# Second-level factors of w_out formed on the chip in the first group of tokens, and two levels in all five products of the second group

## The chip, the cores and the metric

The kernel runs on one core of one Trainium2 chip. The metric is the device time of one execution in microseconds (us), as the median of several executions; lower is better. TensorE is called PE here, VectorE DVE, ScalarE ACT, GpSimd POOL and SyncE SP. Each engine takes its instructions in order. POOL and SP have little arithmetic in this kernel: they issue DMA transfers.

## The reference

The attention block turns q, k and v of shape (4, 8, 768, 64) into tokens x of shape (3072, 512). Two matrix products with a pointwise function between them follow:

```python
def reference(q, k, v, lam, moe_w_in, moe_w_out):
    attn_out = _attn_ref(q, k, v, lam)          # causal, decayed by lam ** distance, state carried from block to block
    x = attn_out.transpose(0, 2, 1, 3).reshape(B * S, H * D)     # (3072, 512)
    h = x @ moe_w_in                            # (512, 2048)
    g = h - np.tanh(h)
    return (g @ moe_w_out).astype(np.float32)   # (2048, 512)
```

Everything is float32 on the chip. The weights arrive as 64-bit floats and are rounded on the chip.

## The kernel before

**Groups.** The 3072 tokens are worked off in NG = 6 groups of 512 (128 positions of each of the 4 batches). Group 0 is the "first group" and group 1 the "second group". For each group there is an attention part (`att_transpose`, `att_scores`, `att_out`, `att_state`), the product with w_in ("up", four column blocks u = 0 to 3), and the product with w_out ("down"). The attention of group g + 1 is put in pieces between the up and down products of group g.

**Seven products instead of eight.** Up and down split their matrices in 2 x 2 blocks and use a seven-product scheme: sums and differences of blocks ("factors") are multiplied, and the products, numbered 1 to 7, are added up. For w_out the seven factors are B11, B21, B22 and the differences T1 to T4. One first-level down product is `down` at L644 to L685: 16 matmuls of 128x128 by 128x256 (the `nc.tensor.matmul` at L655). A "two-level" down product, `down_twice` at L697 to L730, applies the same scheme once more inside a product: seven sub-products of four matmuls of 128x128 by 128x128 (L708), 28 in all, with the sums of the hidden values made by `sums_twice` (L692 to L694) and the sums of w_out's factor made ahead of time. The function `twice(g, n)` says which products have two levels. Before the change these are products 5 and 6 in group 1, and 5, 6, 4, 7 and 3 in groups 2 to 4 (in group 5 all of these but 3).

**Where the factors lie.** w_out is loaded once, in pairs of 128-row blocks, kt = 0 to 7 (`weights`, `round_block`), at the end of group 0's up part and during its down part. For each kt `sums_out` (L252 to L267) makes T1, T2, T3 and T4 on DVE, stores all seven first-level factors to a DRAM tile `factors`, and stores those second-level factors that are plain slices (sub-products 1, 2 and 3) to a DRAM tile `fine`. The tile that holds a pair is one of two `wst` buffers or, for every third pair, `ws` tiles that group 0 does not need (`pair_tiles`). Sub-products 5, 6, 7 and 4 need differences between column halves and between rows of kt even and kt odd. They are made later: `load_quarters` fetches four quarters of a first-level factor from `factors`, and `factors_twice` (L603, L604) makes four 128x512 differences on DVE and stores each to `fine`. This happens for two of the five products between the steps of group 1's up part, and for the other three in group 2's up part.

**The stream of weights.** From group 1 on `piece` loads each factor piece (256 KB) from `factors` or `fine` by a DMA from POOL, RING = 7 pieces ahead.

**The pools that matter for the change.** The natural (token by channel) loads of k rotate through 3 buffers with tag "k" and those of v through 4 buffers with tag "v" in the pool `io`; SP issues them (L131). From group 2 on SP also issues q and k in blocks (L143), 16 transfers for each of the four batches and each of q and k, behind the natural loads on the same queue; DVE transposes them (L319). In the built program each DMA from POOL also waits until the eighth transfer before it on that queue has landed.

**Group 0's down part.** `down_first` (L792) walks over kt and adds all seven products of one pair in seven PSUM banks. `sums_late` (L798, L799) makes, on DVE, the two hidden sums that products 6 and 3 need, after products 1 and 2 of that kt have read the old values. Products 5, 4 and 7 stand between. Ahead of it the attention of group 1 for batches 2 and 3 runs: PE makes the scores (L340), DVE masks them into `ss` (L344), and PE makes `op` (L388, L394) and the state update `kv` (L362).

Of the kernel before, what the change touches and what calls it, by code (L numbers as in the profile page):

```python
# [9 lines left out]
F32 = mybir.dt.float32  # L10
# [6 lines left out]
AL = mybir.AluOpType  # L17
# [7 lines left out]
def kernel(  # L25
# [32 lines left out]
    nc = tc.nc  # L58
# [6 lines left out]
    NG = S // BLK  # L65
    HB = GRP // 2
    NU = DFF // 512
# [7 lines left out]
    io = ctx.enter_context(tc.tile_pool(name="io", bufs=4))  # L75
# [3 lines left out]
    opool = ctx.enter_context(tc.tile_pool(name="opool", bufs=4))  # L79
# [43 lines left out]
    raw, late = {}, {}  # L123
# [54 lines left out]

    ws = [wpool.tile([128, 3, 2, 256], F32, name=f"ws_{u}") for u in range(NU)]

    NX = 7
    factors = dram.tile([NX, 128, KH, 256], F32, name="factors")

    SUB = (1, 2, 6, 5, 7, 3, 4)
# [37 lines left out]
    def weights(n):  # L222

        while ready["done"] < min(n, len(blocks)):
            at_ = ready["done"]
            load_weights(at_ + WAHEAD)
            kind, n_, m = blocks[at_]
            if kind == "out" and m == 0:
                pair[n_] = pair_tiles(n_)
            w = w1[n_][:, m] if kind == "in" else pair[n_][0][:, 2 * m:2 * m + 2]  # L230
            if at_ in wraw:
                round_block(w, wraw.pop(at_), at_ < 2 * KI)
            else:
                load_block(nc.gpsimd, w, kind, n_, m)
            ready["done"] += 1

    def pair_tiles(kt):

        if kt % 3 == 2:
            return tuple(ws[u].rearrange("p x k c -> p (x k) c")[:, 0:4] for u in (3, 2))  # L240
        wt = wst.tile([128, 8, 256], F32, name="wt", tag="w")
        return wt[:, 0:4], wt[:, 4:8]

    def sums_in(u):
        a11, a12, a21, a22 = (w1[u][:, 2 * c:2 * c + 2, r] for r, c in ((0, 0), (0, 1), (1, 0), (1, 1)))
# [3 lines left out]
            tc.keep_in_program_order(nc.vector.tensor_tensor(dst, x, y, op=op))  # L249

    def sums_out(kt):
        bt, tt = pair[kt]  # L252
        b11, b12, b21, b22 = (bt[:, x] for x in range(4))
        t1, t2, t4, t3 = (tt[:, x] for x in range(4))
        nc.vector.tensor_tensor(t1, b12, b11, op=AL.subtract)
        nc.vector.tensor_tensor(t2, b22, t1, op=AL.subtract)
        nc.vector.tensor_tensor(t3, b22, b12, op=AL.subtract)
        nc.vector.tensor_tensor(t4, b21, t2, op=AL.subtract)
        f = factors[:].rearrange("x p k c -> p x k c")
        nc.gpsimd.dma_start(out=f[:, 0:1, kt, :], in_=bt[:, 0:1, :])  # L260
        nc.gpsimd.dma_start(out=f[:, 1:3, kt, :], in_=bt[:, 2:4, :])
        nc.gpsimd.dma_start(out=f[:, 3:NX, kt, :], in_=tt[:, 0:4, :])

        for x, j in ((1, 0),) if kt % 2 == 0 else ((2, 0), (3, 1)):
            dst = fine[:, SUB.index(x), :, kt // 2, :].rearrange("n p c -> p n c")
            nc.gpsimd.dma_start(out=dst[:, 0:1], in_=bt[:, 3:4, ts(j, 128)])
            nc.gpsimd.dma_start(out=dst[:, 1:5], in_=tt[:, 0:4, ts(j, 128)])  # L267

    def round_block(w, raw64, first):

# [276 lines left out]
    RING = 7  # L547

    def twice(g, n):
        return n in TWICE and not (g == NG - 1 and n == 3) and not (g == 1 and n in (4, 7, 3))  # L550

    def in_turn(g):

# [5 lines left out]
    def pieces_of(g):  # L559
        if g >= GI:  # L560
            yield from ((g, ("in", 4), x) for x in (6, 5, 3))
        if g == 2:
            yield from ((g, ("quarter", t), x) for t in (2, 3, 4) for x in range(4))
        for n in (1, 2, 4, 5, 6, 7):
            yield from ((g, n, x) for x in (SUB if twice(g, n) else range(NU)))
        if g == NG - 1:
            yield from ((g, 3, x) for x in range(NU))
            return
        for kind, x in in_turn(g):
            if kind == "down":  # L570
                yield g, 3, x
            elif x in (3, 5, 6):
                yield g + 1, ("in", 2), x
# [1 line left out]
    stream = [x for g in range(1, NG) for x in pieces_of(g)]  # L575
    sent = {"n": 0}

    MADE = (5, 6, 4, 7, 3)
    quarters = {}

    def quarter_source(t, i, j):
        return factors[XAT[FACT[MADE[t]][1]]].rearrange("p (u m) c -> p u m c", m=2)[:, :, i, ts(j, 128)]

    def load_quarters(t):

        for i in range(2):
            for j in range(2):
                if t > 1:
                    quarters[t, i, j] = piece(2, ("quarter", t), 2 * i + j).rearrange("p m (v c) -> p (m v) c", v=2)
                    continue  # L590
                if t == 0:
                    x = late["pool"].tile([128, NU, 128], F32, name="wq", tag="wb", bufs=RING)
                else:
                    x = opool.tile([128, NU, 128], F32, name="oq", tag="o")
                nc.gpsimd.dma_start(out=x, in_=quarter_source(t, i, j))
                quarters[t, i, j] = x

    def factors_twice(t):

        b11, b12, b21, b22 = (quarters.pop((t, i, j)) for i in range(2) for j in range(2))  # L600
        t1, t2, t4 = (late["pool"].tile([128, NU, 128], F32, name=f"wt{x}", tag="sums", bufs=4) for x in (1, 2, 4))
        for x, dst, a, b in ((5, t1, b12, b11), (6, t2, b22, t1), (7, b12, b22, b12), (4, t4, b21, t2)):
            tc.keep_in_program_order(nc.vector.tensor_tensor(dst, a, b, op=AL.subtract))  # L603
            nc.gpsimd.dma_start(out=fine[TWICE.index(MADE[t]), SUB.index(x)], in_=dst)  # L604
            yield

    def piece(g, n, x):

        i = stream.index((g, n, x))
        while sent["n"] < min(i + RING, len(stream)):  # L610
            g_, n_, x_ = stream[sent["n"]]
            t = late["pool"].tile([128, 2, 256], F32, name="wb", tag="wb", bufs=RING)
            if isinstance(n_, tuple) and n_[0] == "quarter":
                nc.gpsimd.dma_start(out=t.rearrange("p m (v c) -> p (m v) c", v=2),
                                    in_=quarter_source(n_[1], *divmod(x_, 2)))
            elif isinstance(n_, tuple):
                nc.gpsimd.dma_start(out=t.rearrange("p m c -> p (m c)"), in_=fine_in[
                    INNER.index(n_[1]), (5, 6, 3).index(x_)].rearrange("p u c -> p (u c)"))
            elif twice(g_, n_):
                nc.gpsimd.dma_start(out=t.rearrange("p m c -> p (m c)"),  # L620
                                    in_=fine[TWICE.index(n_), SUB.index(x_)].rearrange("p u c -> p (u c)"))
            else:
                nc.gpsimd.dma_start(out=t, in_=factors[XAT[FACT[n_][1]]][:, 2 * x_:2 * x_ + 2, :])  # L623
            blks[stream[sent["n"]]] = t
            sent["n"] += 1
        return blks.pop((g, n, x))
# [146 lines left out]

    acc = {}
    ACC = {1: ("ya", 1), 2: ("w", 1), 5: ("z", 1), 6: ("yb", 1), 7: ("att", 4), 4: ("att", 4), 3: ("att", 4)}
    FIRST = {1: (11, 0, 0), 2: (21, 0, 2), 3: (21, 0, 3), 4: (22, 1, 2), 5: ("S1", 1, 0), 6: (11, 1, 1), 7: (12, 1, 3)}

    def sums_first(u):
        g11, g12, g22, s1 = (hidden(0, c)[:, u] for c in (11, 12, 22, "S1"))
# [96 lines left out]
    for kt in range(KH):  # L876
        down_first(kt, (1, 2))
        if kt + 1 < KH:
            sums_out(kt + 1)
        sums_late(kt)  # L880
        down_first(kt, (5, 4, 7, 6, 3) if kt + 1 < KH else (5, 6, 7, 4, 3))
        if kt + 3 < KH:
            weights(ready["done"] + 2)
        if kt == 2:
            sums_in(1)
# [3 lines left out]
    late["pool"] = ctx.enter_context(tc.tile_pool(name="late", bufs=1))  # L889


    turns = {1: (0, ((0, 7), (1, 14))), 2: (7 * NU, ((2, 1), (3, 5), (4, 9)))}
    made, making = [], {}
    load_quarters(0)
    load_quarters(1)
    up(1, 0, 1)
    for g in range(1, NG):
        last = g == NG - 1
        p0, p1 = attention(g + 1) if not last else ([], [])
        for u in range(NU):  # L900
            for n in (2, 6, 5, 7, 1, 4, 3) if g < GI else (1, 7, 3) if u == 0 else (6, 5, 1, 7, 3) if u + 1 < NU else (
                    6, 5, 7, 1, 3):
                if n != 1:
                    up(g, u, n)
                elif u + 1 < NU:
                    up(g, u + 1, 1)
                else:
                    every(down(g, 1))
                if g == 1 and u < 2 and n == 5:
                    sums_in(u + 2)  # L910
                if g in turns:
                    made.append(n)
                    step = len(made) - turns[g][0]
                    for t, first in turns[g][1]:
                        if step == first:
                            if t > 1:
                                load_quarters(t)
                            making[t] = factors_twice(t)
                        if first <= step < first + 4:
                            next(making[t])  # L920
            if g == GI - 1:
                inner_weights(u)
            if not last and u > 1:
                run(p0[u - 2:u - 1])
# [65 lines left out]
```

## Time and profile before

| what | value |
|---|---|
| median of 3 runs | 669.5 us (668.18 to 673.25) |
| the profiled execution: time, span in the profile | 669.39 us, 667.6 us |
| PE busy, matmuls | 655.6 us (98%), 4920 |
| DVE busy | 466.4 us (70%) |
| ACT, POOL busy | 213.7 us, 210.8 us (32% each) |
| bytes moved by DMA | 128.82 MB |
| group 0's down part (L792) on PE | 98.53 to 146.98 us |
| group 1: up from 146.98, down part from 204.31 us | |
| group 2: up from 273.04, down part from 312.47 us | |

A program matmul shows as two PE records in the trace. A line of the timeline gives the start in us, the length in us, engine, line of the kernel, operation, destination and sources, and the count of merged records; in brackets stands how long the engine had been idle before it, and what ended that.

### The profile page before, as it was taken

The page shows a single profiled execution, that of the slowest core. Times are in us where ns is not written, and L with a number is a line of the kernel's source. Part 1 is how long each engine was busy: PE and PEld are TensorE (multiplying, and loading weights), DVE is VectorE, ACT ScalarE, POOL GpSimd, SP SyncE. Part 2 cuts the span into 40 slices and gives each one's busy share as a digit, 9 for nine tenths or more (in the row PEclk, how much of TensorE's full clock was granted, in tenths as well). Part 3 has the DMA queues.
Part 4 walks back from the last instruction along what each step waited for, and adds up shares of the span by engine and source line. Part 5 has one row for each costly group of instructions (what it writes and reads, how often), then busy time and mean ns, then how long its engine had stood idle before and what let it go on. Part 6 is the DMA issues. An engine that isn't in the chain of part 4 may idle for free.

```text
span 667.6 us, 13061 instructions
## 1 busy us (share of the span) xinstructions
PE 655.6 (98%) x4920; PEld 594.1 (89%) x4920; DVE 466.4 (70%) x839; ACT 213.7 (32%) x402; POOL 210.8 (32%) x365
## 2 busy tenths in 40 slices
PE   7899999999999999999999999999999999999998
PEld 6688888888888989888999988999988899988897
DVE  4467896746988762599885379987368877357753
ACT  4787935503321112341112343112233112234110
POOL 0001445734522433254436101344300245400251
PEclk9999999999999999999999999999999999999999
DMA  9999988958855977568889533698730677610495
GB/s 209 223 201 261 286 306 234 342 160 233 229 133 137 235 188 205 150 198 259 239 260 280 142 76 75 170 274 255 215 70 17 158 237 219 219 37 0 120 295 170
DMA packets 163038, 128.82 MB, mean 193 GB/s; under 512 B 134176, under 2 KB 135328, under 8 KB 162976
## 3 DMA queue, kind: packets, MB, share of 16 engines
q0 software_dynamic: 29296, 96.49, 45.0%
q1 hardware_dynamic: 133536, 31.50, 24.0%
q8 instruction: 39, 0.64, 0.4%
q14 instruction: 23, 0.19, 0.1%
q10 hardware_dynamic: 144, 0.00, 0.0%
HBM read 103.55 MB, written 24.38 MB: 192 GB/s over the span
## 4 chain that ended last, share of the span: by engine, by line
PE 79%; issue 9%; DMA 5%; POOL 2%; SPq 2%; ACT 1%; DVE 1%; DVEq 0%; POOLq 0%; ACTq 0%
PE y L446 12%; PE y L708 10%; PE acc L792 7%; PE zw L708 7%; PE h L763 7%; PE z L446 7%; PE w L655 4%; PE y L655 4%; PE y L530 4%; PE plain L655 3%; PE sp L340 3%; PE op L394 3%; PE z L530 2%; DMA wb<-fine 2%; PE op L388 1%
## 5 line engine op out<-in xcount | busy, mean ns | idle before, releaser
L620 POOL DMA_DIRECT2D wb<-fine x147 | 79.4, 541 | 113.7 <-PE y L708 50.6
L623 POOL DMA_DIRECT2D wb<-factors x56 | 30.4, 543 | 155.9 <-PE y L655 99.7
L454 ACT ACTIVATE th<-g 128x512 f32<-128x512 f32 x76 | 47.7, 632 | 99.1 <-DVE g L459 33.2
L446 PE MATMUL y<-xt,w 128*128 128x256 f32 x320 | 74.0, 380 | 0.0
L446 PEld LDWEIGHTS y<-xt,w 128*128 128x128 f32 x320 | 59.9, 190 | 8.5 <-ACT g L534 0.9
L711 ACT ACTIVATE q<-y 128x128 f32<-128x128 f32 x84 | 23.3, 278 | 130.8 <-PE y L708 130.0
L455 DVE TENSOR_TENSOR g<-g,th 128x512 f32<-128x512 f32 x76 | 51.9, 688 | 16.8 <-ACT th L454 16.7
L763 PE MATMUL h<-xt,w 128*128 128x256 f32 x256 | 58.0, 383 | 2.3 <-DVE w L284 2.3
L763 PEld LDWEIGHTS h<-xt,w 128*128 128x128 f32 x256 | 47.7, 190 | 10.2 <-DVE w L284 2.6
L708 PE MATMUL y<-wb,g 128*128 128x128 f32 x384 | 51.1, 278 | 0.0
L708 PEld LDWEIGHTS y<-wb,g 128*128 128x128 f32 x384 | 46.4, 192 | 1.1 <-issue 0.3
L446 PE MATMUL z<-tt,ws 128*128 128x256 f32 x160 | 38.0, 380 | 0.0
L446 PE MATMUL z<-xt,ws 128*128 128x256 f32 x160 | 37.9, 380 | 0.0
L446 PE MATMUL y<-tt,ws 128*128 128x256 f32 x160 | 37.8, 379 | 0.0
L655 PE MATMUL y<-wb,g 128*128 128x256 f32 x160 | 35.6, 379 | 0.7 <-DVE g L465 0.7
L655 PE MATMUL w<-wb,g 128*128 128x256 f32 x160 | 35.8, 382 | 0.0
L344 DVE TENSOR_TENSOR ss<-sp,mask 128x512 f32<-128x512 f32 x48 | 31.1, 684 | 6.3 <-PE sp L340 6.3
L205 POOL DMA_DIRECT2D raw<-in_moe_w_out_dram x16 | 8.8, 549 | 84.7 <-ACT r L281 66.2
L655 PEld LDWEIGHTS y<-wb,g 128*128 128x128 f32 x160 | 30.3, 190 | 5.1 <-PE y L446 1.0
L446 PEld LDWEIGHTS z<-xt,ws 128*128 128x128 f32 x160 | 30.3, 190 | 4.3 <-ACT g L462 0.2
L655 PEld LDWEIGHTS w<-wb,g 128*128 128x128 f32 x160 | 30.1, 190 | 4.4
L708 PE MATMUL zw<-wb,g 128*128 128x128 f32 x256 | 33.8, 275 | 0.0
(198 smaller groups left out, 1349.6 us busy)
## 6 DMA issues: line engine op xcount, KB each, us to landing
wb<-fine POOLq DMA_DIRECT2D x147, 256.0 KB, 4.0
wb<-factors POOLq DMA_DIRECT2D x68, 256.0 KB, 4.2
raw<-in_moe_w_out_dram POOLq DMA_DIRECT2D x16, 512.0 KB, 5.8
v_nat<-in_v_dram SPq DMA_DIRECT2D x24, 256.0 KB, 5.2
fine<-wt POOLq DMA_DIRECT2D x24, 256.0 KB, 4.7
wb<-fine_in POOLq DMA_DIRECT2D x24, 256.0 KB, 4.2
k_nat<-in_k_dram SPq DMA_DIRECT2D x20, 256.0 KB, 4.9
raw<-in_moe_w_in_dram SPq DMA_DIRECT2D x8, 512.0 KB, 6.5
```

What stands on the lines that cost most here:

```text
L344: tied(g == 0, nc.vector.tensor_tensor(ss[:, j], sp[j], mask[:, j], op=AL.mult))
L446: nc.tensor.matmul(out=t[:, m, :], lhsT=wt[:, kt, ts(m, 128)], rhs=x[:, kt, :], start=first and m == 0 and kt == 0, stop=kt == 1, skip_gro ...
L454: nc.scalar.activation(th, src, AF.Tanh)
L455: nc.vector.tensor_tensor(dst(c), src, th, op=AL.subtract)
L530: nc.tensor.matmul(out=dst[:, ts(u, 128)], lhsT=a, rhs=b, start=x in (1, 2, 5) and u == 0, stop=True, skip_group_check=True)
L620: nc.gpsimd.dma_start(out=t.rearrange("p m c -> p (m c)"), in_=fine[TWICE.index(n_), SUB.index(x_)].rearrange("p u c -> p (u c)"))
L623: nc.gpsimd.dma_start(out=t, in_=factors[XAT[FACT[n_][1]]][:, 2 * x_:2 * x_ + 2, :])
L655: nc.tensor.matmul(out=t[:, m, :], lhsT=a[:, u, kt, ts(m, 128)], rhs=wb[:, kt, :], start=first and u == 0 and m == 0 and kt == 0, stop=u = ...
L708: nc.tensor.matmul(out=dst, lhsT=a[:, u, :], rhs=wb[:, ts(u, 128)], start=x in (1, 2) and u == 0, stop=u == NU - 1, skip_group_check=True)
L711: nc.scalar.activation(keep, dst, AF.Copy)
L763: tied(u == 0, nc.tensor.matmul(out=hm[c][:, m, :], lhsT=w1[u][:, i, a, ts(m, 128)], rhs=xt[0, t][:, i, :], start=m == 0 and i == 0, stop= ...
L792: nc.tensor.matmul(out=acc[n][:, r, :], lhsT=a[:, ts(r, 128)], rhs=b, start=kt == 0 and r == 0, stop=kt == KH - 1, skip_group_check=True)
```

## The change

- `factors` keeps three of seven planes (B11, B21, B22): the one-level products left after group 0 are 1 and 2, and 3 in group 5, and they read no others.
- `pair_tiles` orders the pair's tile so that B21, B22, T1, T2, T4, T3 lie next to each other, and `sums_out` stores with fewer and larger DMAs.
- A new function `sums_fine(u)` makes the second-level factors 5, 6, 7 and 4 for all five products from the pairs kt = 2u and 2u + 1 while both are on the chip: for each of the four factors one 128x128 and one 128x4x128 difference on DVE and a store of each to `fine`. Its results are put in buffers that rotate with the natural k and v loads (tags "k" and "v" of `io`).
- `load_quarters`, `factors_twice`, the "quarter" pieces of the stream and the calls of them in groups 1 and 2 go.
- `twice` now says yes for products 4, 7 and 3 of group 1.

```diff
-    NX = 7
+    NX = 3
...
-            w = w1[n_][:, m] if kind == "in" else pair[n_][0][:, 2 * m:2 * m + 2]
+            w = w1[n_][:, m] if kind == "in" else pair[n_][m][:, 0:2]
...
     def pair_tiles(kt):
         if kt % 3 == 2:
-            return tuple(ws[u].rearrange("p x k c -> p (x k) c")[:, 0:4] for u in (3, 2))
+            x, y = (ws[u].rearrange("p x k c -> p (x k) c") for u in (3, 2))
+            return x[:, 0:2], y[:, 0:6]
         wt = wst.tile([128, 8, 256], F32, name="wt", tag="w")
-        return wt[:, 0:4], wt[:, 4:8]
+        return wt[:, 0:2], wt[:, 2:8]
...
     def sums_out(kt):
-        bt, tt = pair[kt]
-        b11, b12, b21, b22 = (bt[:, x] for x in range(4))
-        t1, t2, t4, t3 = (tt[:, x] for x in range(4))
+        x, y = pair[kt]
+        b11, b12, b21, b22, t1, t2, t4, t3 = (t[:, i] for t, n in ((x, 2), (y, 6)) for i in range(n))
...
-        nc.gpsimd.dma_start(out=f[:, 0:1, kt, :], in_=bt[:, 0:1, :])
-        nc.gpsimd.dma_start(out=f[:, 1:3, kt, :], in_=bt[:, 2:4, :])
-        nc.gpsimd.dma_start(out=f[:, 3:NX, kt, :], in_=tt[:, 0:4, :])
+        nc.gpsimd.dma_start(out=f[:, 0:1, kt, :], in_=x[:, 0:1, :])
+        nc.gpsimd.dma_start(out=f[:, 1:NX, kt, :], in_=y[:, 0:2, :])
 
-        for x, j in ((1, 0),) if kt % 2 == 0 else ((2, 0), (3, 1)):
-            dst = fine[:, SUB.index(x), :, kt // 2, :].rearrange("n p c -> p n c")
-            nc.gpsimd.dma_start(out=dst[:, 0:1], in_=bt[:, 3:4, ts(j, 128)])
-            nc.gpsimd.dma_start(out=dst[:, 1:5], in_=tt[:, 0:4, ts(j, 128)])
+        for n, j in ((1, 0),) if kt % 2 == 0 else ((2, 0), (3, 1)):
+            nc.gpsimd.dma_start(out=fine[:, SUB.index(n), :, kt // 2, :].rearrange("n p c -> p n c"),
+                                in_=y[:, 1:6, ts(j, 128)])
+
+    def sums_fine(u):
+
+        (b11, b12), (b21, b22) = (tuple(pair[2 * u + i][1][:, 1:6, ts(j, 128)] for j in range(2)) for i in range(2))
+        one = io.tile([128, 4, 1, 128], F32, name="f1", tag="k", bufs=3)
+        parts = [(0, 1, [one[:, x] for x in range(4)]),
+                 (1, 5, [io.tile([128, 4, 128], F32, name="f4", tag="v", bufs=4) for _ in range(4)])]
+        for x, a, b in ((5, b12, b11), (6, b22, 5), (7, b22, b12), (4, b21, 6)):
+            for lo, hi, t in parts:
+                dst = {5: t[0], 6: t[1], 7: t[2], 4: t[3]}
+                nc.vector.tensor_tensor(dst[x], a[:, lo:hi], dst[b] if isinstance(b, int) else b[:, lo:hi],
+                                        op=AL.subtract)
+                nc.gpsimd.dma_start(out=fine[lo:hi, SUB.index(x), :, u, :].rearrange("n p c -> p n c"), in_=dst[x])
...
-        return n in TWICE and not (g == NG - 1 and n == 3) and not (g == 1 and n in (4, 7, 3))
+        return n in TWICE and not (g == NG - 1 and n == 3)
...
-        if g == 2:
-            yield from ((g, ("quarter", t), x) for t in (2, 3, 4) for x in range(4))
...
-    def load_quarters(t):
...
-    def factors_twice(t):
-        b11, b12, b21, b22 = (quarters.pop((t, i, j)) for i in range(2) for j in range(2))
...
-            tc.keep_in_program_order(nc.vector.tensor_tensor(dst, a, b, op=AL.subtract))
-            nc.gpsimd.dma_start(out=fine[TWICE.index(MADE[t]), SUB.index(x)], in_=dst)
...
         down_first(kt, (5, 4, 7, 6, 3) if kt + 1 < KH else (5, 6, 7, 4, 3))
+        if kt % 2 == 0:
+            sums_fine(kt // 2)
         if kt + 3 < KH:
             weights(ready["done"] + 2)
...
-    load_quarters(0)
-    load_quarters(1)
     up(1, 0, 1)
...
-                            if t > 1:
-                                load_quarters(t)
-                            making[t] = factors_twice(t)
-                        if first <= step < first + 4:
-                            next(making[t])
```

## The prediction

> **What bounds the kernel.** First the page: busy shares, then the chain of work that ended last.
>
> ```profile
> span 667.6 us, 13061 instructions
> ...
> PE 655.6 (98%) x4920; PEld 594.1 (89%) x4920; DVE 466.4 (70%) x839; ACT 213.7 (32%) x402; POOL 210.8 (32%) x365
> ...
> PE 79%; issue 9%; DMA 5%; POOL 2%; SPq 2%; ACT 1%; DVE 1%; DVEq 0%; POOLq 0%; ACTq 0%
> ```
>
> PE is busy 98% of the span: whatever shortens its stream is gained, whatever makes it wait is lost. The table of 10 us stretches shows idle PE only in the first 70 us, between 290 and 300 us (0.67 us) and between 430 and 440 us (0.76 us). Second, PE's timeline in group 1's down part prices a one-level and a two-level product, and shows one of those gaps.
>
> ```profile
> 204.31 7.17 PE L655 MATMUL w<-wb,g 128*128 128x256 f32 x32
> ...
> 215.28 7.17 PE L655 MATMUL plain<-wb,g 128*128 128x256 f32 x32
> 222.29 1.05 PE L708 MATMUL y<-wb,gS 128*128 128x128 f32 x8
> ...
> 228.64 2.06 PE L340 MATMUL sp<-qt,kt 64*128 64x128 f32 x32
> ...
> 298.23 0.67 PE L655 MATMUL y<-wb,g 128*128 128x256 f32 x2 [0.67 <-DVE g L465]
> ```
>
> Third, the end of group 0's up part, where the new work goes: DVE, then POOL, then PE.
>
> ```profile
> 83.91 1.35 DVE L771 TENSOR_TENSOR g<-h,th 128x512 f32<-128x512 f32 x2
> ...
> 91.20 1.28 DVE L344 TENSOR_TENSOR ss<-sp,mask 128x512 f32<-128x512 f32 x2
> ...
> 92.99 1.28 DVE L344 TENSOR_TENSOR ss<-sp,mask 128x512 f32<-128x512 f32 x2
> 95.41 0.69 DVE L771 TENSOR_TENSOR g<-h,th 128x512 f32<-128x512 f32 x1 [1.14 <-ACT th L770]
> ...
> 101.15 0.42 DVE L798 TENSOR_TENSOR g<-gS,g 128x256 f32<-128x256 f32 x1
> ```
>
> ```profile
> 78.29 0.54 POOL L205 DMA_DIRECT2D raw<-in_moe_w_out_dram  x1 [1.25 <-ACT r L281]
> ...
> 85.67 0.55 POOL L266 DMA_DIRECT2D fine<-wt  x1 [1.37 <-DMA raw<-in_moe_w_out_dram]
> ```
>
> ```profile
> 94.67 1.10 PE L388 MATMUL op<-qd,state 64*64 64x128 f32 x32
> ...
> 98.53 1.99 PE L792 MATMUL acc<-wt,g 128*128 128x256 f32 x8
> ```
>
> DVE has no gap from 79.84 to 94.2 us: any stall there reaches `ss`, and PE starts L388 only 2.19 us after the first `ss` pair is done (94.67 against 92.48). The stores of `fine` (L267) that POOL issued between 75 and 100 us landed after:
>
> ```profile
> DMA to landing us min/median/max: 5.2/6.0/7.1
> ```
>
> **What is removed.** *Products 4, 7 and 3 of group 1.* One one-level product takes 222.29 - 215.28 = 7.01 us, one two-level product 228.64 - 222.29 = 6.35: 0.66 less, 2.0 for three. Measured whole, group 1's down part takes 68.73 us (204.31 to 273.04) and group 2's, with all five, 66.91 (312.47 to 379.38): -1.8. Group 3's, with a 0.76 us wait for wb<-fine in it, takes 67.35 (417.87 to 485.22): -1.4. I take -1.8. *The quarters.* 20 differences (0.60 us apart), 20 loads and 20 stores of 256 KB go. In group 1 they cost PE nothing (no gap there). Group 2's up part takes 39.43 us (273.04 to 312.47), group 3's without them 38.49 (379.38 to 417.87): -0.9. Gain: 2.7, at least 2.3.
>
> **What is added in group 0.** DVE gets 16 differences of 512 elements (0.60 us from start to start) and 16 of 128 (0.20, L503's spacing): 12.8 us. In the 40 us from 100 to 140 DVE is busy 25.5, so the sum fits. POOL gets 60 stores in place of 48, about 1 MB more, at 32% busy: hidden, except where it is named below. What costs is order. In the built program the first eight differences of `sums_fine(0)` stand among the DVE work of 80 to 90 us, and only two buffers of tag "v" are free then (the others hold v for batches 2 and 3 of group 1). So the third large difference (x = 7) waits until the *store of the first* (x = 5) has landed, and behind it on DVE stand a g difference, qd, the factors of w_in and the four `ss`.
>
> - *When that store goes.* It is the eighth transfer after the raw load of 78.29, whose landing releases POOL at 85.67. Without that wait POOL would reach it at about 84.45. So 85.7, earliest 84.45.
> - *When it lands.* 6.0 us later, the median above: 91.7 (bounds 84.45 + 5.2 = 89.65 and 85.7 + 7.1 = 92.8). DVE, with 2.5 us of new differences behind it, gets there at 86.4 and stalls 5.3.
> - *What is late.* The difference takes 0.6, then the work that began at 84.51 (the second of L771's two) follows at 92.3: 7.8 late. Less the 2.19 us of cover, PE starts L388 5.6 us late (bounds 3.5 and 6.7). Late next is `sums_late(0)`: three more new differences (1.4 us) come ahead of it, the gaps of 1.6 us before it are used up, and it ends 7.55 late, at 109.1. PE wants it for product 6, at 98.53 + 5 x 0.865 + 5.6 = 108.45: 0.7 more. Sum 6.3 (bounds 4.2 and 7.4).
> - *Later in group 0.* `sums_fine(1)` puts six stores, 3.9 us of issuing, ahead of the raw load that L205 issues at 114.47; it goes 1.9 us later relative to PE. ACT waits for that load already (2.55 us at 121.19), so the rounding for kt = 6 and, behind it on DVE, `sums_late(4)` come late: 0.5 us of PE (bounds 0 and 1.5).
>
> Of the Trainium skill's "DMA: Bandwidth & Descriptors", section "Anatomy of one DMA — SWDGE (gpsimd) path", the fit is 2.0 us plus the bytes at 436 GB/s, an estimate of 2.6 us for 256 KB. The rows say 5.2 to 7.1, in a stretch where the queues are full (330 GB/s). By the fit the wait would cost PE 2.9 in all instead of 6.3, and the kernel would end at about 670.0. The skill's page "SBUF — State Buffer" warns, under its table of doors, that DVE's two-port modes lock POOL out of writing descriptors, which would speak against more DVE work beside more POOL DMAs. L267's issue took 0.75 us in the midst of DVE's busiest stretch as elsewhere, so by the row nothing is added, and the sum has no term for it.
>
> **SP's queue.** The natural loads of k and v for group 2 now come after `sums_fine`'s buffers, and wait for its last stores; behind them on SP stand the blocks of q and k, which begin at 132.46 today.
>
> ```profile
> 132.46 9.45 SPq L143 DMA_DIRECT2D q_blk<-in_q_dram  x16
> ...
> 198.42 8.02 SPq L143 DMA_DIRECT2D k_blk<-in_k_dram  x16
> ```
>
> Group 0's last eight stores issue until about 148 and land some 4.7 us later (the median from 100 to 145), so SP starts at about 153. Eight sets took 74 us: the last ends at 227 and lands (3.5) at 230.5. Product 4 then begins at 215.28 + 6.8 = 222.1 and ends, with two levels, at 228.4; in the built program DVE transposes batches 2 and 3 after it, the last k block at about 231, in the midst of product 5. Covered, with nothing to spare: cost 0, up to 3.
>
> **Sum.** -2.7 + 6.3 + 0.5 = +4.1 us on the span of 667.6, so 671.7; with the 1.8 us around it (669.39 - 667.6) 673.5. The profiled execution is 0.1 below the median of 669.5, so the sum is used as it is: 673.5. By the bounds: +4.2 - 2.7 = +1.5 to +7.4 + 1.5 - 2.3 = +6.6, or 671 to 676.
>
> **Rivals.**
> - *The wait is covered.* If x = 7's buffer is free before DVE needs it, or PE has other cover, only the gain is left: 669.4 - 2.7 = 666.7. For it: DVE's total fits. Against it: the named buffers, the full DVE row and 5.2 us as the shortest landing.
> - *SP's blocks come too late (slower).* One set of 16 took 8.0 to 12.1 us; the sets of 149.9 to 181 took 10.2 on average. If eight sets average over 9.3 us, the last k block lands after 231, DVE stands at its transposition (L319), and PE at product 5, whose last steps need DVE. At 10 us a set this costs about 5: 678.5. For it: the stream wb<-fine runs beside it at the end. Against it: the quarters' transfers are gone from the same stretch.
> - *Two levels in group 1 gain nothing.* Seven pieces of 256 KB a product in place of four, each used up in 0.89 us; the gap at 436 us was such a wait. If each product waits 0.7, 1.8 of gain is lost: 675.3.
>
> **How the numbers follow.** The first case 58%, the wait covered 17%, SP late 20%, nothing gained in group 1 5%. What a measurement of this kernel can tell from no change is about 1%, 6.7 us (the three runs spread over 0.76%). Faster by more than that would need a gain that no row shows: 3%. Over 676.2 lies the SP case and a part of the first: 25%. Within: 72%. The range reaches from the covered wait, 666.5, to 680, SP at 10 us a set with the first wait at its upper bound.
>
> **What would show it.** Right: on DVE a gap of about 5 us before the third 128x512 row of `sums_fine`, put down to a DMA fine<-f4; L388 at about 100.3; group 0's down part from 104 to 154; group 1's down part shorter by 1.8; no gap near 298. Wrong: no such gap, or L388 at 95; a DVE wait for k_blk near 231; gaps on wb<-fine in group 1; a chain that leaves PE elsewhere.

## The result, and the profile after

| kernel | median | executions | ratio to the kernel before, 95% interval |
|---|---|---|---|
| before | 669.5 us (668.18 to 673.25) | 9 | |
| changed | 676.26 us (672.46 to 677.37) | 9 | 1.0084 (1.0064 to 1.0103) |
| changed, in a second set of runs | 673.63 us (672.41 to 676.11) | 8 | 1.0059 (1.0039 to 1.0078) |

By the ratios the change costs 0.6 to 0.8%, some 4 to 5.6 us; the medians differ by 6.8 us (1.0%) in the first set and by 3.9 us in the second. It is slower for certain, as both intervals leave 1 out. By the ratios that is less than the 1% that the prediction set as its bound; the median of the first set lies just at the bound (676.26 against 676.2). The profiled execution is the fastest of its nine (672.46 us, span 670.7 us), so the profile shows 3.1 us more span than before, not the whole loss; what the others had besides comes under the experiments.

The page first:

```profile
span 670.7 us, 13240 instructions
...
PE 654.7 (98%) x4992; PEld 594.8 (89%) x4992; DVE 477.8 (71%) x869; ACT 215.2 (32%) x413; POOL 199.0 (30%) x346
...
PE 69%; issue 11%; DMA 7%; DVE 5%; ACT 3%; POOL 3%; SPq 2%; POOLq 0%; DVEq 0%; ACTq 0%
```

PE is busy 0.9 us less than before in a span that is 3.1 us longer, and its share of the chain falls from 79 to 69%: the added time is waiting. Next DVE and POOL at the end of group 0's up part (start, length, engine, line, operation; in brackets the idle time before it and what ended that). `sums_fine`'s subtraction is L276 here, its store L278, `ss` L355.

```profile
82.11 0.68 DVE L276 TENSOR_TENSOR f<-wt 128x512 f32<-128x512 f32 x1
...
85.63 0.43 DVE L258 TENSOR_TENSOR ws<-ws 128x256 f32<-128x256 f32 x1
89.31 0.69 DVE L276 TENSOR_TENSOR f<-wt 128x512 f32<-128x512 f32 x1 [3.25 <-DMA fine<-f]
...
96.53 1.27 DVE L355 TENSOR_TENSOR ss<-sp,mask 128x512 f32<-128x512 f32 x2
```

```profile
84.79 1.31 POOL L278 DMA_DIRECT2D fine<-f  x2 [0.34 <-DVE ws L257]
```

DVE stands still for 3.25 us until the store that POOL issued at 84.79 has landed (4.5 us), and the first pair of `ss` ends 5.3 us later than before (96.53 + 1.27 = 97.80 against 92.48). What PE makes of it:

```profile
97.26 0.43 PE L399 MATMUL op<-qd,state 64*64 64x128 f32 x2 [2.58 <-DVE ss L355]
97.86 1.10 PE L399 MATMUL op<-qd,state 64*64 64x128 f32 x30 [0.17 <-DVE ss L355]
98.89 1.97 PE L405 MATMUL op<-ss,v_nat 128*64 128x128 f32 x32
100.69 1.10 PE L373 MATMUL kv<-v_nat,k_nat 128*64 128x64 f32 x32
...
107.13 3.72 PE L769 MATMUL acc<-wt,g 128*128 128x256 f32 x16 [0.82 <-DVE g L775]
...
133.13 1.99 PE L769 MATMUL acc<-wt,g 128*128 128x256 f32 x8 [1.54 <-DVE g L775]
...
233.57 1.13 PE L685 MATMUL y<-wb,gS 128*128 128x128 f32 x8 [1.42 <-DMA wb<-fine]
```

Four places: `op` (L399) waits for `ss`; product 6 of kt = 0 and of kt = 4 wait for `sums_late` (L775); product 5 of group 1 waits for a piece of the stream. A gap in the down part costs a little more than itself: the row after it starts 0.17 us later than the gap says (1.73 us separate such rows of eight; 104.41 + 1.73 + 0.82 = 106.96, not 107.13) and lasts 0.11 us longer to the next start (3.56 against 3.45), 0.28 in all. Lengths of the stages on PE, in us, from the starts of their first rows:

| stage | before | changed | changed, second profile |
|---|---|---|---|
| group 0's down part begins | 98.5 | 101.7 | 101.8 |
| group 0, down part | 48.4 | 51.4 | 51.7 |
| group 1, down part | 68.7 | 68.6 | 67.6 |
| group 2, up part | 39.4 | 38.5 | 38.5 |
| group 2, down part | 66.9 | 66.4 | 66.4 |
| group 3, down part | 67.3 | 66.4 | 66.4 |

On SP the blocks of q and k of group 2 begin at 154.26, in place of 132.46:

```profile
154.26 13.57 SPq L143 DMA_DIRECT2D q_blk<-in_q_dram  x16
...
215.84 9.25 SPq L143 DMA_DIRECT2D k_blk<-in_k_dram  x16
```

### The profile page after: what moved, and what is told of

It reads as the page before. It is cut to its first block, busy times and chain, and to the rows that moved or that the text cites. A ratio compares the mean times of both kernels' runs of the same rounds, so it can differ in the third digit from the quotient of the medians.

```text
span 670.7 us, 13240 instructions
## 1 busy us (share of the span) xinstructions
PE 654.7 (98%) x4992; PEld 594.8 (89%) x4992; DVE 477.8 (71%) x869; ACT 215.2 (32%) x413; POOL 199.0 (30%) x346
## 4 chain that ended last, share of the span: by engine, by line
PE 69%; issue 11%; DMA 7%; DVE 5%; ACT 3%; POOL 3%; SPq 2%; POOLq 0%; DVEq 0%; ACTq 0%
PE y L457 12%; PE y L685 12%; PE zw L685 9%; PE z L457 8%; PE y L541 4%; PE w L632 4%; PE y L632 4%; PE acc L769 3%; DMA raw<-in_moe_w_in_dram 3%; PE sp L351 2%; PE z L541 2%; PE op L405 2%; SPq L210 1%; DMA fine<-f 1%; PE op L399 1%
## 5 line engine op out<-in xcount | busy, mean ns | idle before, releaser
L597 POOL DMA_DIRECT2D wb<-fine x168 | 90.5, 539 | 138.2 <-PE y L685 61.8
L688 ACT ACTIVATE q<-y 128x128 f32<-128x128 f32 x96 | 26.6, 277 | 149.5 <-PE y L685 148.5
L600 POOL DMA_DIRECT2D wb<-factors x44 | 23.8, 542 | 170.1 <-PE y L632 127.8
L685 PE MATMUL y<-wb,g 128*128 128x128 f32 x456 | 60.6, 278 | 0.0
L685 PEld LDWEIGHTS y<-wb,g 128*128 128x128 f32 x456 | 55.1, 192 | 1.3 <-issue 0.3
L685 PE MATMUL zw<-wb,g 128*128 128x128 f32 x304 | 40.3, 275 | 0.1
L685 PEld LDWEIGHTS zw<-wb,g 128*128 128x128 f32 x304 | 37.0, 192 | 0.3 <-DVE g L690 0.3
L769 PE MATMUL acc<-wt,g 128*128 128x256 f32 x144 | 33.2, 381 | 2.4 <-DVE g L775 2.4
L355 DVE TENSOR_TENSOR ss<-sp,mask 128x512 f32<-128x512 f32 x48 | 31.0, 682 | 5.8 <-PE sp L351 5.8
L632 PEld LDWEIGHTS y<-wb,g 128*128 128x128 f32 x160 | 30.4, 190 | 4.1
```

The costliest lines, as they stand in the source:

```text
L355: tied(g == 0, nc.vector.tensor_tensor(ss[:, j], sp[j], mask[:, j], op=AL.mult))
L632: nc.tensor.matmul(out=t[:, m, :], lhsT=a[:, u, kt, ts(m, 128)], rhs=wb[:, kt, :], start=first and u == 0 and m == 0 and kt == 0, stop=u = ...
L685: nc.tensor.matmul(out=dst, lhsT=a[:, u, :], rhs=wb[:, ts(u, 128)], start=x in (1, 2) and u == 0, stop=u == NU - 1, skip_group_check=True)
L688: nc.scalar.activation(keep, dst, AF.Copy)
L769: nc.tensor.matmul(out=acc[n][:, r, :], lhsT=a[:, ts(r, 128)], rhs=b, start=kt == 0 and r == 0, stop=kt == KH - 1, skip_group_check=True)
```

## The experiments

Kernels that were run as one set share a chip and its runs of the kernel before; the ratios are to those. The theory at the start: DVE's wait for a buffer costs most, by the buffers that `sums_fine` shares with the k and v loads.

**Buffers of its own, for all pairs (e1), the first pair (e2), the others (e3).**

```diff
 # e1; e2 has f4 of its own for u == 0 alone, e3 f1 and f4 for u > 0 alone
-        one = io.tile([128, 4, 1, 128], F32, name="f1", tag="k", bufs=3)
+        one = work.tile([128, 4, 1, 128], F32, name="f1", tag="th")
+        if u % 2 == 0:
+            four = [opool.tile([128, 4, 128], F32, name="f4", tag="o") for _ in range(4)]
+        else:
+            two = [work.tile([128, 2, 4, 128], F32, name="f4", tag="ss") for _ in range(2)]
+            four = [two[i][:, j] for i in range(2) for j in range(2)]
...
```

> The results of sums_fine get buffers that no k or v load uses, for all four pairs of row blocks. This takes away both waits that the changed kernel added: DVE's wait for the landing of a store before the third large difference, and SP's wait for the last stores before group 2's loads. All four large differences of the first pair then stand ahead of ss on DVE (4 x 0.69 = 2.8 us of work against the 2.19 us of cover). Theory (buffers): no DVE gap near 89; L399's first matmul at about 95 to 96 in place of 97.26; group 2's blocks begin on SP at about 132 in place of 154.26; the span falls by 2 to 4 us in all, the median to about 673 to 674. Rival 1 (work, not buffers: the added differences and stores cost their time wherever they stand): L399 stays at 97 or later, median 676. Rival 2 (SP's late blocks were what made the stream of weights wait in product 5 of group 1): group 1's down part falls from 68.6 to about 66.9 as well, and the median to about 671 to 672.

> Only the first pair's large results get buffers of their own; the other three pairs stay in the buffers of the k and v loads, so SP's loads for group 2 still wait until about 148. Theory (DVE's wait costs PE): L399 at about 96, 1 to 1.5 us earlier than in the changed kernel; SP's blocks still begin at about 153; median 1 to 2 us under the changed kernel's, 674.5 to 675.5. Rival (the wait was only the form of it, DVE is late by its added work): no difference from the changed kernel.

> The first pair's results stay in the buffers of the k and v loads (DVE's wait for the store of x = 5 stays, about 3 us); the other three pairs get buffers of their own, so SP is not held up by the last stores. Theory (SP's lateness makes the wait in product 5 of group 1): L399 as in the changed kernel, 97.3; SP's blocks of group 2 begin at about 132; group 1's down part 66.9 in place of 68.6, no gap on wb<-fine; median 674.5. Rival (the stream of seven pieces for a product is too much by itself): the gap of about 1.4 us on wb<-fine stays, the down part stays at 68.6, median 676.

Measured: e1 670.36 us, ratio 0.999 (0.9967 to 1.0014); e2 671.7 us, 1.0007 (0.9987 to 1.0028); e3 675.52 us, 1.0067 (1.0046 to 1.0088). DVE's wait is gone in e1 and e2. The first pair's buffers alone take away nearly all of the loss; the others' leave it. That is more than either theory gave, and more than the profiles show at L399: it began at 96.41 in e1 and 96.01 in e2, only 0.85 and 1.25 us before the changed kernel's. These times understate it, since the executions had not come equally far before: PE's last wait for `w` in group 0's up part ended at 68.15 in the changed kernel, 69.17 in e1, 68.42 in e2 and 68.35 in the kernel before. Counted from there, `op` begins after 26.3 us in the kernel before, 29.1 in the changed kernel (29.6 in its second profile), 27.2 in e1 and 27.6 in e2, and 26.5 to 27.2 in the four later kernels with buffers of their own (e6, e7, e8, e11): the buffers give back 1.5 to 3.1 us of some 3. The medians say more: 0.8 to 0.9% against the first set of the changed kernel, 0.5 to 0.7% against the second. One thing that can add to it stands in e3's profile, of a usual execution (676.07 us). It has the wait of the changed kernel (3.56 us on DVE), and this on PE, where L407, L413 and L381 are the changed kernel's L399, L405 and L373:

```profile
99.67 2.57 PE L407 MATMUL op<-qd,state 64*64 64x128 f32 x32 [2.89 <-DVE ss L363]
102.18 3.68 PE L413 MATMUL op<-ss,v_nat 128*64 128x128 f32 x32
```

The same 32 matmuls that took 1.97 us now take 3.68. The table of stretches has PE's granted clock, as a part of full speed, as the number after the five engines (then the share of DMA and GB/s):

```profile
98.00:99.00 1.00, 0.00 (x0) 0.00 (x0) 1.00 (x3) 0.00 (x0) 0.00 (x0) 1.00 0.18 70
99.00:100.00 1.00, 0.33 (x2) 0.29 (x2) 1.00 (x3) 0.00 (x0) 0.00 (x0) 0.50 0.00 0
...
104.00:105.00 1.00, 1.00 (x12) 1.00 (x10) 1.00 (x3) 0.00 (x0) 0.23 (x1) 0.50 1.10 271
...
106.00:107.00 1.00, 1.00 (x31) 0.93 (x26) 0.90 (x2) 0.51 (x1) 0.75 (x1) 1.00 0.00 0
```

From 99.0, inside PE's wait, to 105.8 the clock is at half: 6.8 us. From L407's start to the down part's it takes 7.09 us, against 4.46 in the changed kernel's profile: 2.6 us. Part of it is given back, since the 0.82 us wait of product 6 that follows is covered then.

As for SP: in e3 the blocks of group 2 began at 143.5 and in e1 at 137.9 (not at 132, as expected), in e2 at 152.0. In e3 the gap on wb<-fine in group 1 is gone, as rival 2 of e1 had it, but a gap of 0.77 us behind DVE stands there instead, and the part takes 67.7, not 66.9. e1 and e2 differ by 1.3 us, with intervals that overlap: SP's lateness costs between nothing and 1.3. All the profiles together point to how it reaches PE. In the six in which the blocks begin between 152.0 and 157.6 (the changed kernel twice, e2, and e5, e7 and e10 below) PE waits for wb<-fine in group 1's down part, 0.36 to 1.42 us in all; in the five with the same products in which they begin between 133.9 and 143.5 (e1, e3, and e6, e8 and e11 below, the last two with eight pieces ahead) no such wait is listed, but waits of 0.55 to 1.15 us behind DVE. So an early SP takes the gap away and yet gains little: the part takes 67.6 to 68.6 us with late blocks and 67.5 to 68.0 with early ones.

**Filling the wait (e5, e10) beside the changed kernel (e9).**

```diff
+        if g == 1 and bs[0] == 2:
+            warm = bank("idle", "ya", 1)
+            for _ in range(10):
+                nc.tensor.matmul(out=warm[:, 0:128], lhsT=ident, rhs=ident, start=True, stop=True)
```

> The changed kernel with ten matmuls of 128x128 that nothing reads (the identity by itself, into a free bank), put on PE between the last h of group 0 and L399, where PE waits about 2.7 us for ss; some 2.2 us of work in that gap. Everything else is the changed kernel. Theory (the wait is paid twice: first as idle time, then by a lower granted clock): the timed executions of the changed kernel show a mean granted clock of 0.995 to 0.997, which is 4 to 7 us at half clock and 2 to 3.4 us of time; with the gap filled the clock stays at 1.0 and the median falls from 676.3 to about 673. Rival (the granted clock has nothing to do with the gap, or the lower means are noise): the same median, 676 or more, and clocks as before.

> The changed kernel as it is, once more, beside the next one on the same chip, for a second profile of it: its first profile is of the fastest of nine executions and shows full granted clock, the other eight show 0.995 to 0.997. Theory (clock): the profile or most executions show one stretch of 3.4 or 6.8 us at half clock from the wait before L399 on; median 676. Rival: the low means come from elsewhere (the first 15 us, as in one execution of the kernel with filling matmuls), and the clock at L399 is 1.0.

> The changed kernel with ten unused matmuls in the wait before L399, once more, now beside the changed kernel on the same chip, since its first median (676.5, six executions) was not lower though four of the six had the full clock. Theory (half clock costs 1.7 to 3.4 us): 2 us or more under the changed kernel of the same call. Rival (the half clock falls on matmuls that PE would have waited behind anyway, or the filling costs as much): no difference, within 1 us.

Measured: e5 676.48 us, 1.0083 (1.0061 to 1.0106); e9 673.63 us and e10 675.22 us in one set, 1.0059 (1.0039 to 1.0078) and 1.0081 (1.0058 to 1.0104). The filling did what it was to do, and did not help:

```profile
94.37 2.39 PE L391 MATMUL idle<-ident 128*128 128x128 f32 x20
97.42 0.43 PE L403 MATMUL op<-qd,state 64*64 64x128 f32 x2 [0.66 <-DVE ss L355]
98.02 1.10 PE L403 MATMUL op<-qd,state 64*64 64x128 f32 x30 [0.17 <-DVE ss L355]
```

The gap fell to 0.66 us, the clock at `op` is full, and 8 of the 12 executions have a mean granted clock of 1.0 where the changed kernel has 0.995 or 0.997 in 14 of 17. By e9's expectation the mean clock was to be low in most executions (it was, in six of eight), but the profile drew one at full clock, with a gap of 2.89 us like e3's. e10's profile begins the down part at 101.88 against e9's 101.77, and loses 0.54 us more in it and 2.4 us on waits for wb<-fine in groups 1 to 3, against e9's 0.4; e5's profile has 3.3 us of such waits. Why the stream waits more there was not found.

So what the half clock is worth stays open. For it: the three executions of the changed kernel with a mean clock of 0.999 or 1.0 took 672.41 to 672.92 us, the 14 others 673.46 to 677.37; e1 and e2, without the long gap, show 1.0 or 0.999 in 22 of 24, and the kernel before in 80 of the 93 executions run beside e1 to e12, while e3, with the gap, shows 0.995 or 0.997 in 11 of 12. Against it: e5 and e10, whose eight executions at 1.0 still took 674.61 to 677.71 us. That a wait of about 2.9 us on PE can be followed by half clock is shown (e3), and that low means are more frequent with the gap; that this is the difference between the changed kernel's profile and its median is not shown.

**One level again in group 1 (e4).**

```diff
 # e4, on e1
-XAT = {"B11": 0, "B21": 1, "B22": 2, "T1": 3, "T2": 4, "T4": 5, "T3": 6}
+XAT = {"B11": 0, "B21": 1, "B22": 2, "T4": 0, "T3": 1}
...
-        return n in TWICE and not (g == NG - 1 and n == 3)
+        return n in TWICE and not (g == NG - 1 and n == 3) and not (g == 1 and n in (4, 7, 3))
```

> As the kernel with buffers of its own throughout, but products 4, 7 and 3 of group 1 are one-level again, as before the change; they load planes B11 and B21 in place of T4 and T3, so that the traffic is that of the kernel before and no plane has to be stored for it, and the values of group 1 are not the reference's. Theory (two levels save 0.6 us a product where the stream keeps up): group 1's down part 68.7 against 66.9 in the two-level form, median 1.8 us over that kernel's. Rival (in group 1 two levels gain nothing, since the stream of pieces waits): the same time within 0.5 us.

Measured: 672.13 us, 1.0017 (0.9998 to 1.0036), 1.8 us over e1, as the theory said, though the intervals overlap; group 1's down part took 68.72 us against 67.67 in e1, a gain of 1.05 and not 1.8. The other 0.7 of the medians is not in this stage: in e4's profile PE also waits longer for wb<-fine in groups 3 and 5 (1.12 and 1.44 us).

**What holds up product 6 of kt = 4: POOL's order (e6, e7) or DVE's (e11).** In e6 `sums_fine` of pairs 2 and 3 reads tiles that hold the next values already, so that those factors are made of other data with the same work.

```diff
 # e6, on e1
+        if kt + 3 < KH:
+            weights(ready["done"] + 2)
         if kt % 2 == 0:
             sums_fine(kt // 2)
-        if kt + 3 < KH:
-            weights(ready["done"] + 2)
 # e7, on e1: in sums_fine
-                nc.gpsimd.dma_start(out=fine[...], in_=dst[x])
+                nc.sync.dma_start(out=fine[...], in_=dst[x])
```

> As the kernel with buffers of its own throughout, with sums_fine called after the next pair's rounding in place of before it, so that the raw loads of the pair kt = 6 go ahead of the six stores of sums_fine(1) on POOL. Theory (the raw load of 114.3 to 120.9 behind the stores makes sums_late(4) late): the PE gap of 1.54 us at 131.92 goes, group 0's down part from 51.6 to about 50 us, median 668.5 to 669. Rival (DVE's own backlog, busy without a pause from 122.4 to 131.5, makes it late): the gap stays within 0.4 us of 1.54, median 670.4.

> As the kernel with buffers of its own throughout, with the stores of sums_fine issued by SP in place of POOL. POOL's queue then has the raw loads of pairs 3 to 7 in the same order as before the change, and DVE has the same work. SP's loads of group 2 stand behind the last stores again, at about 150. Theory (POOL's queue): the gap at kt = 4 shrinks to under 0.5 us, group 0's down part to about 49.5 to 50; SP's lateness costs up to 1.3 us (what the kernel with own buffers for the first pair alone was slower); median 669 to 670. Rival (DVE's backlog): the gap of 1.5 us stays and the median is 671 to 672.

Measured: e6 669.79 us, 0.9982 (0.9966 to 0.9998); e7 673.26 us, 1.0045 (1.0024 to 1.0065). In e7 POOL's queue was free of those stores, and its raw loads went earlier, yet the wait was the same to the hundredth:

```profile
124.34 1.13 PE L773 MATMUL acc<-wt,g 128*128 128x256 f32 x4 [1.64 <-DVE g L779]
125.88 2.86 PE L773 MATMUL acc<-wt,g 128*128 128x256 f32 x12 [0.41 <-DVE g L780]
...
132.86 1.99 PE L773 MATMUL acc<-wt,g 128*128 128x256 f32 x8 [1.54 <-DVE g L779]
```

It also got a new one of 1.64 us, and lost. In e6, where the differences stand elsewhere on DVE, the gap split into 0.75 and 0.72 us. So the rival held: DVE's own order. In the changed kernel DVE is busy without a pause from 123.62 on, and both roundings of the pair kt = 6 stand ahead of `sums_late(4)`.

**Eight pieces ahead in the stream (e8), and the sums of w_in moved (e11).**

```diff
 # e8, on e1
-    RING = 7
+    RING = 8
 # e11, on e8
-        if kt == 2:
+        if kt == 5:
             sums_in(1)
```

> As the kernel with buffers of its own throughout, with eight pieces of weights ahead in the stream in place of seven. Theory (single late landings: one more piece, 0.9 us of PE work, covers them): no wait on wb<-fine above 0.2 us in groups 1 to 5, group 1's down part from 67.7 to about 66.6, group 2's from 67.2 to 66.4, median about 669. Rival (in those stretches the queues deliver less than PE uses, so that any depth runs empty): the waits stay, same median within 0.5 us.

> Buffers of its own for sums_fine, eight pieces ahead in the stream, and the four sums of w_in's second column block (2.7 us of DVE work at 123 to 127) moved from kt = 2 to kt = 5. The gap before product 6 of kt = 4 was 1.54 us in all kernels whose DVE order was the same, whatever POOL did. Theory (DVE's backlog): with 2.7 us less work ahead, that gap goes, group 0's down part falls from 51.5 to about 49.7, median 668. Rival (a raw load or ACT sets the end of the rounding): the gap stays within 0.3 us of 1.54, or goes elsewhere, median 669.7.

Measured: e8 669.75 us, 0.9982 (0.9963 to 1.0001); e11 668.09 us, 0.9969 (0.9953 to 0.9985). In e8's profile one wait on wb<-fine is left, of 0.47 us, in the last group; group 1's down part did not shorten (67.96), as gaps of 0.34 and 0.77 us behind DVE stand there. In e11 the gap of kt = 4 is gone:

```profile
126.79 3.62 PE L773 MATMUL acc<-wt,g 128*128 128x256 f32 x16
130.24 1.89 PE L773 MATMUL acc<-ws,g 128*128 128x256 f32 x8
```

```profile
126.13 0.55 DVE L298 TENSOR_SCALAR wt<-wt 128x512 uint32<-128x512 uint32 x1
126.60 0.41 DVE L779 TENSOR_TENSOR g<-gS,g 128x256 f32<-128x256 f32 x1
```

PE goes from kt = 4 to kt = 5 without idle time, as the half of `sums_late(4)` that product 6 needs is done at 127.0 (131.9 in e1). Group 0's down part takes 49.1 us, 2.5 less than in e1. The move also made the scheduler put that half behind the first rounding in place of the second, so the 2.7 us and the new order acted together. That the median fell with it is not shown apart: the intervals of e8 and e11 overlap.

**The control (e12): eight pieces in the kernel before.**

```diff
-    RING = 7
+    RING = 8
```

> The kernel before the change with eight pieces ahead in the stream of weights in place of seven, and nothing else: a control for the version that beat both kernels (668.1, ratio 0.9969), which has three edits on top of the change. Theory (that version's gain is the change's own, -2.7 us less small waits, set free by the buffers and the order on DVE): the deeper stream alone gives 0.5 us at most here, whose profile has waits of 0.76 and 0.26 us on wb<-fine; median 669 to 670. Rival (the gain comes from the deeper stream): median 668.2 or less, ratio 0.997.

Measured: 667.95 us (five executions) against 671.09 in that set, 0.9955 (0.9941 to 0.9968). The rival held: with the deeper stream alone, the kernel before is as fast (0.9955 against 0.9969, with intervals that overlap) as the changed kernel with it and two more edits (e11). So no run that computes the reference's values shows a gain of the change over the kernel before at equal depth; e6, with other data in two pairs, comes nearest (upper bound 0.9998). What e11's own gain comes from is less clear: on the changed kernel's side the deeper stream brought nothing that stands out of the noise (0.9982 in e8, 0.999 in e1).

## Why the prediction was right or wrong

The forecast (673.5 us, within 1%) came out, and partly by luck: the two medians, 676.26 and 673.63, lie 2.8 and 0.1 us over it, and its sum has errors that cancel. On the profiled execution, whose span grew by 3.1 us where the sum said 4.1:

- *The wait for a buffer.* Place and mechanism as predicted: the third large difference, for the store of the first. The step that was mis-sized is "when it lands": 6.0 us was the median of the old stores; this one took 4.5, and it went at 84.8 and not 85.7. The stall was 3.25 and not 5.3 (3.56 to 4.05 in the four other profiles that have it: e3, e5, e9, e10), `op` 2.6 late and not 5.6, and the down part, which begins behind it, 3.2. With product 6 of kt = 0 (predicted 0.7, measured 0.82, and 0.28 to start again) the term is 3.2 + 1.1 = 4.3 in place of 6.3, at the lower bound. The estimate by the fit of the Trainium skill's "DMA: Bandwidth & Descriptors", section "Anatomy of one DMA — SWDGE (gpsimd) path", 2.6 us, would have been 1.9 us too low where the row was 1.5 us too high.
- *Later in group 0.* Mis-sized and wrongly explained: 0.5 (at most 1.5) was predicted through the raw load behind six stores; it was 1.54 + 0.27 = 1.8. e7 took the stores off POOL and the gap stayed; e11 changed DVE's order and it went.
- *SP's queue.* Blocks at 154.3 (153 predicted), the last set's end at 225.1 (227). No wait for k_blk came, as predicted, and e1 and e2 put the cost at 1.3 at most; but by the profiles above the lateness did reach PE, by a way that the prediction names only as an argument for a rival: through the stream wb<-fine beside the late blocks, 1.42 us in the profile.
- *Products 4, 7 and 3 of group 1.* The term that failed on the gain side: 1.8 predicted, 0.1 and 1.1 in the two profiles, 1.05 by e4 and e1. Gaps on wb<-fine in group 1, which the prediction lists as a sign of being wrong, are what took it, 1.42 us at 233.57. They are the third rival's waits, but not by its cause: two levels alone have none where SP is early, and there waits behind DVE took 0.55 to 1.15.
- *The quarters.* Group 2's up part 38.5: 0.9, as predicted, and no gap near 298.
- *Not in the sum.* Groups 2, 3 and 5 got 0.5, 0.9 and 0.5 us shorter in the down part. In groups 3 and 5 waits on wb<-fine of the execution before (0.76 and 0.26 us) did not come again; in group 2 no wait is listed, but in product 5 of the kernel before the sub-products stand 0.89 to 1.07 us apart, and 0.89 to 0.91 in all but one place now. I had taken 66.91 us as the price of a down part with five two-level products; without waits it is 66.4.

Together: +4.3 + 1.8 - 0.1 - 0.9 - 1.9 = +3.2. The prediction also took the profiled execution to stand for the median. Of the kernel before it did; of the changed kernel it lay 3.8 us under it in the first set of runs and 0.7 in the second. No term said what a wait of some 3 us does to PE's clock.

## What to carry to other kernels

Before new work borrows the buffers of another pool, look up which of them are still held when it starts, and who stands in line behind the first instruction that must wait: here one difference held up masks, `op` and the state. Price such a wait by its own landing, and read the order of the engine itself before blaming the queue that feeds it. And run the control: the repaired change beat the kernel before only with one more piece ahead in the stream, and the kernel before gains as much from that piece alone.

## What the runs showed of the hardware

- After a PE wait of 2.89 us the granted clock was 0.50 for 6.8 us in e3, and 1.0 after the same 2.89 us in e9 and after 2.58 us in the changed kernel's first profile. In e5 it was 0.5 once for 3.4 us, from 7.8 to 11.2. The Trainium skill's "TensorE: Matmul & The Clock Gate", "Part 1: The HAM clock gate (the "warmup" mystery)", has the clock fall to half after one idle window of about 3.4 us; the lengths here are one and two of those, but here a shorter wait was followed by half clock in one execution and not in two others.
- Eight pieces of 256 KB ahead in place of seven, where PE uses one in 0.89 us, made the kernel before 0.45% faster, though its profile showed only 1.0 us of waits for pieces; with eight, the down parts of groups 2, 3 and 5 are 0.5, 0.6 and 0.5 us shorter in the profile. Such waits differ between executions of one kernel: one of 1.42 us in group 1 in the changed kernel's first profile, three of 0.36, 0.45 and 0.18 us in groups 1 and 5 in its second.
